# Column-normalised attention with a soft mixture of experts: the last half tile of each batch filled up to 128 partitions

## The chip, the cores and the metric

The kernel runs on one core of one Trainium2 chip. The metric is the device time of one execution in microseconds (us). Of three runs of the kernel before, the median is 304.97 us, the lowest 303.45, the highest 307.35. The time of a kernel is compared with that of the kernel before on the same chip.

## The reference

There are four batches (B) of q, k and v, each with N = 5056 rows and C = 256 columns. In each batch q and k are normalised by column, their product over the rows gives a 256 x 256 matrix, and v times its softmax is the attention's output. That goes through a soft mixture of 8 experts with 4 slots each, whose softmax over rows runs over all batches.

```python
def _attn_ref(q, k, v, tau):
    qn = q / (np.linalg.norm(q, axis=1, keepdims=True) + 1e-06)
    kn = k / (np.linalg.norm(k, axis=1, keepdims=True) + 1e-06)
    s = kn.transpose(0, 2, 1) @ qn / tau
    s = s - s.max(-1, keepdims=True)
    a = np.exp(s)
    a /= a.sum(-1, keepdims=True) + 1e-09
    return (v @ a).astype(np.float32)

def _moe_ref(x, phi, w1, w2):
    logits = x @ phi
    d = softmax of logits over all rows
    slot_input = (d.T @ x).reshape(E, S_per_e, D)
    for e in range(E):
        h = np.maximum(slot_input[e] @ w1[e], 0.0)
        slot_out[e] = h @ w2[e]
    c = softmax of logits over the 32 slots
    return (c @ slot_out).astype(np.float32)
```

Here x is the attention's output of all batches, 20224 rows. 5056 is 39 x 128 + 64: the last tile of 128 rows in a batch is half full.

## The kernel before

**Tiles.** A batch is cut into UB = 10 units of 512 rows for q and k, and into PB = 5 pieces of 1024 rows for v and the output. A unit lies in SBUF as a tile raw of [128 partitions, 4 row tiles, q and k, 256 columns], 1 MB, of which there are five buffers. A piece of v is [128, 8 row tiles, 256], also 1 MB, loaded in two halves of 512 KB. Rows fill the tiles in order, so in the last unit of a batch the fourth row tile has 64 rows instead of 128, and in the last piece of v the eighth.

**Stages.** First, unit by unit: load_qk loads raw; cast (ACT) and low (DVE) split two of its four row tiles into a high and a low part (tile hl); score (PE) adds the products of k and q to two PSUM banks S, with L252 for row tiles read straight from raw and L258 and L259 for split ones; square (ACT) writes the squares to a tile sq, and add (DVE) adds them to the batch's first sq. After a batch's last unit, att_sums and what follows turn the sums into norms, and the softmax a and a small matrix M are made. Meanwhile, piece by piece of the batch before: load_v and load_vt load v and, for some pieces, its transpose; turn (PE) transposes the others; logits, exps, weights and gather run the softmax over rows and gather the slot inputs. Then the experts' weights w1 and w2 are loaded, and up, relu, flip_h, back_h and down run the experts. At the end, piece by piece, out_mul (PE) makes the output in PSUM, out_evict copies it to a tile o of 1 MB (even banks ACT at L791, odd banks DVE at L793), and store writes it to HBM.

**Order.** Every step is entered in a plan, and a list of numbers written out by hand, ORDER, says in what order the steps are given out. Each engine runs its own instructions in that order. All loads and stores are issued on one queue, SP's.

**The half tiles.** The last unit of q and k comes from arrays of its own: L128 loads three row tiles of 128 rows (768 KB, from qk3), L129 the 64 rows (128 KB, from qkh, into partitions 0 to 63 of the fourth). The last half piece of v is loaded by L143 (three row tiles, 384 KB) and L145 (64 rows, 64 KB). The square of such a unit is two instructions (L226 for three row tiles, L227 for the 64 rows), and so is its last sum (L234 and L235). The matmuls of score, gather and turn take `pc = HD` rows there, with HD = 64. In the output the rows of a piece are permuted, so that the half tile of the last piece stands in the first 96 partitions of two of the eight row tiles; out_evict puts these two in the last places of o, and store writes six row tiles of 128 partitions (L804, 768 KB) and two of 96 (L805, 192 KB). The output in HBM is one flat array with a part for full pieces, one for the six and one for the two row tiles; the host puts the rows in order.

Of the kernel before, what the change touches and what calls it, by code (L numbers as in the profile page):

```python
# [8 lines left out]
F32 = mybir.dt.float32  # L9
F32R = mybir.dt.float32r  # L10
AF = mybir.ActivationFunctionType
ALU = mybir.AluOpType
# [3 lines left out]
B, N, C = 4, 5056, 256  # L16
P, S, G = 128, 32, 4
UB = 10
PB = 5
UT = 512  # L20
# [61 lines left out]
def colnorm_attention_soft_moe(  # L82
    ctx: ExitStack,
    tc: tile.TileContext,
    qk: bass.AP,
    qk3: bass.AP,
    qkh: bass.AP,
    v8: bass.AP,
    v7: bass.AP,
    vh: bass.AP,  # L90
    vt8: bass.AP,
    vt7: bass.AP,
    few: bass.AP,
    w1: bass.AP,
    w2: bass.AP,
    oa: bass.AP,
    ob6: bass.AP,
    oh: bass.AP,
):
# [19 lines left out]
    raws, sqs = {}, {}  # L119

    def load_qk(u, parts=((0, 4),)):
        b, i = divmod(u, UB)
        raw = apool.tile([P, 4, 2, C], F32, tag="raw", name=f"raw{u}", bufs=NRAW)
        if i < UB - 1:
            for lo, hi in parts:
                sp.dma_start(raw[:, lo:hi], qk[b, i][:, lo:hi])
        else:
            sp.dma_start(raw[:, 0:3], qk3[b])  # L128
            sp.dma_start(raw[:HD, 3], qkh[b])  # L129
        raws[u] = raw  # L130

    vs, vts = {}, {}
# [1 line left out]
    def load_v(p, h):  # L134
        b, i = divmod(p, PB)
        if p not in vs:
            vs[p] = slot("v" if p < 17 else "raw", f"v{p}")
        vt = vs[p]
        lo, hi = 4 * h, 4 * h + 4
        if i < PB - 1:  # L140
            sp.dma_start(vt[:, lo:hi], v8[b, i][:, lo:hi])
        else:
            sp.dma_start(vt[:, lo : min(hi, 7)], v7[b][:, lo : min(hi, 7)])  # L143
            if h:
                sp.dma_start(vt[:HD, 7], vh[b])  # L145

    def load_vt(p, m):
        b, i = divmod(p, PB)
# [65 lines left out]
    for b in range(B):  # L214
        sqtag[b * UB] = free[0]
        o = free[1:]
# [3 lines left out]

    def square(u):
        sq = apool.tile([P, 4, 2, C], F32, tag=f"sq{sqtag[u]}", name=f"sq{u}")
        if u % UB < UB - 1:
            act.activation(sq, raws[u], AF.Square)  # L224
        else:
            act.activation(sq[:, 0:3], raws[u][:, 0:3], AF.Square)  # L226
            act.activation(sq[:HD, 3], raws[u][:HD, 3], AF.Square)  # L227
        sqs[u] = sq

    def add(u, lo, hi):  # L230
        b, i = divmod(u, UB)
        a, s = sqs[b * UB], sqs[u]
        if i == UB - 1 and hi == 4:
            dve.tensor_tensor(a[:, lo:3], a[:, lo:3], s[:, lo:3], op=ALU.add)  # L234
            dve.tensor_tensor(a[:HD, 3], a[:HD, 3], s[:HD, 3], op=ALU.add)  # L235
        else:
            dve.tensor_tensor(a[:, lo:hi], a[:, lo:hi], s[:, lo:hi], op=ALU.add)  # L237

    def score(u, j):
        b, i = divmod(u, UB)  # L240
# [511 lines left out]
    ots, ops = {}, {}  # L752
# [21 lines left out]
    def out_evict(b, p, hf, g):  # L774
        if (b, p) not in ots:
            ots[b, p] = slot(OT[b * PB + p], f"o{b}_{p}")
        ot = ots[b, p]
        if p < PB - 1:
            dst = ot.rearrange("p q (w c) -> p (q w) c", w=2).rearrange("p (x gh) c -> p gh x c", x=2)
            dst = dst[:, 2 * g : 2 * g + 2]  # L780
            src = ops[b, p, hf, g]
            if hf is None:
                src = src.rearrange("p h (x c) -> p h x c", x=2)
            else:
                dst = dst[:, :, hf]
        else:
            lo, step = (2 * g, 1) if g < 2 else (g + 2, 2)
            dst = ot[:, lo : lo + step + 1 : step, :]
            src = ops[b, p, hf, g]
        if g % 2 == 0:  # L790
            act.copy(dst, src)  # L791
        else:
            dve.tensor_copy(dst, src)  # L793

    def store(b, p, hf):
        ot = ots[b, p]
        if p < PB - 1:
            o2 = ot.rearrange("p (x q) c -> p x (q c)", x=2)
            if hf is None:
                sp.dma_start(oa[b, p], o2)  # L800
            else:
                sp.dma_start(oa[b, p][:, hf], o2[:, hf])
        else:
            sp.dma_start(ob6[b], ot[:, 0:6])  # L804
            sp.dma_start(oh[b], ot[:96, 6:8])  # L805

    def fill(b, k):
        gp = st[b]["gp"]
# [46 lines left out]
    for p in range(14):  # L855
        k = FV + 2 * p
# [5 lines left out]
        b, gi, x, n = group(p)  # L862
# [11 lines left out]
        if p >= 3:  # L874
            at(k + 0.2, gather, p - 3)
            b, gi, x, n = group(p - 3)
# [8 lines left out]
    for b in range(3):  # L885
        k = UB * (b + 1)
# [47 lines left out]
    for p in (17, 18, 19):  # L934
        at(NU + 0.99, load_v, p, 0)
        at(NU + 0.99, load_v, p, 1)
# [193 lines left out]
```

## Time and profile before

| What | us |
|---|---|
| median of three runs | 304.97 |
| the profiled execution | 304.32 |
| its span, first to last instruction | 302.5 |
| PE busy | 260.6 |
| DVE busy | 233.2 |
| ACT busy | 196.1 |

In the span 110.38 MB were moved by DMA, 365 GB/s in the mean. From HBM 89.29 MB were read, and 20.71 MB were written to it. Q and k are loaded from 0.7 to some 180 us, and the stores run from 247.29 us to the end.

How to read the rows: PE is TensorE (PEld its weight loads), DVE VectorE, ACT ScalarE, POOL GpSimd, SP the engine that issues the DMAs (SPq its queue). "S<-raw" is what an instruction writes and reads, by the program's names; "x4" is a count; "L252" a line of the kernel. What stands in brackets at the end of a row is the time for which the engine was idle just before it, and what ended that idle time. PEclk is the clock granted to TensorE as a share of full speed. The DMA share is the mean busy share of 16 DMA engines, and can read a little over 1 where two transfers overlap on an engine.

### The profile page before, as it was taken

The numbers are of one execution on the slowest core, as the hardware profiler recorded it, in microseconds if no ns is written. First come the engines' busy times: TensorE is split into PE (matmuls) and PEld (weight loads), VectorE is DVE, ScalarE is ACT, GpSimd is POOL, SyncE is SP. The second block draws the span as 40 slices with busy tenths as digits, with TensorE's granted clock in tenths as the row PEclk, the third lists the DMA queues.
The fourth block names the chain that finished last, engine by engine and source line by source line (L and its number), as shares of the span: only waits on it lengthen the run. The fifth ranks groups of instructions, "written<-read, shape, count | busy, mean of one in ns | idle before, by whom it ended". The sixth has DMA issues, their size and how long they took to land. (4 is left out here: it accounts for less than half of the span.)

```text
span 302.5 us, 5958 instructions
## 1 busy us (share of the span) xinstructions
PE 260.6 (86%) x2358; PEld 199.4 (66%) x2358; DVE 233.2 (77%) x387; ACT 196.1 (65%) x290; POOL 28.1 (9%) x18
## 2 busy tenths in 40 slices
PE   4999899999999988998999999999989999984000
PEld 3788687877768874875887687777655588763000
DVE  1599959999989979986999999567887547997000
ACT  2996969798879694675886976366840526865000
POOL 0000002000002403000222000133202030000000
PEclk9999799999999999999999999999999999999555
DMA  6999999999999998799899989699999718999996
GB/s 237 427 430 415 374 405 420 371 389 366 423 398 360 417 390 319 280 356 422 281 407 405 385 310 378 248 351 422 406 347 400 305 71 341 404 422 399 420 430 261
DMA packets 21707, 110.38 MB, mean 365 GB/s; under 512 B 2608, under 2 KB 2864, under 8 KB 13616
## 3 DMA queue, kind: packets, MB, share of 16 engines
q1 hardware_dynamic: 21680, 110.01, 92.4%
q8 instruction: 18, 0.29, 0.4%
q14 instruction: 9, 0.07, 0.1%
HBM read 89.29 MB, written 20.71 MB: 364 GB/s over the span
## 5 line engine op out<-in xcount | busy, mean ns | idle before, releaser
L252 PE MATMUL S<-raw 128*128 128x256 f32 (+1 forms) x328 | 82.4, 391 | 6.4 <-DMA raw<-in_qk_dram 4.8
L237 DVE TENSOR_TENSOR sq<-sq,sq 128x1024 f32<-128x1024 f32 (+1 forms) x59 | 81.2, 1393 | 3.2 <-ACT sq L224 2.3
L224 ACT ACTIVATE sq<-raw 128x2048 f32<-128x2048 f32 x36 | 68.7, 1914 | 14.9 <-DMA raw<-in_qk_dram 9.4
L252 PEld LDWEIGHTS S<-raw 128*128 128x128 f32 (+1 forms) x328 | 60.4, 195 | 17.1 <-DMA raw<-in_qk_dram 5.9
L258 PE MATMUL S<-hl 128*128 128x512 f32 x156 | 64.7, 444 | 1.8 <-DVE hl L208 1.8
L208 DVE TENSOR_TENSOR hl<-raw,hl 128x1024 fp32r<-128x1024 f32 x39 | 49.0, 1271 | 8.4 <-ACT hl L202 8.3
L202 ACT CAST hl<-raw 128x1024 fp32r<-128x1024 f32 x39 | 40.4, 1044 | 7.1 <-DMA raw<-in_qk_dram 4.8
L259 PE MATMUL S<-hl 128*128 128x256 f32 x156 | 44.0, 282 | 0.0
L258 PEld LDWEIGHTS S<-hl 128*128 128x128 f32 x156 | 29.6, 190 | 10.5 <-DVE hl L208 2.6
L259 PEld LDWEIGHTS S<-hl 128*128 128x128 f32 x156 | 29.8, 191 | 0.6
L406 PE MATMUL vTp<-ident,v 128*128 128x128 f32 (+1 forms) x160 | 23.4, 277 | 1.7 <-DMA v<-in_v_dram 1.7
L537 PE MATMUL G<-v,dn 128*32 128x256 f32 (+1 forms) x320 | 23.3, 382 | 0.0
L406 PEld LDWEIGHTS vTp<-ident,v 128*128 128x128 f32 (+1 forms) x160 | 18.2, 141 | 6.7 <-issue 3.0
L764 PE MATMUL op_None<-so,cT 32*128 32x256 f32 x256 | 19.6, 397 | 2.3 <-ACT o L791 1.2
L305 POOL TENSOR_TENSOR rn<-rn,half 128x4 f32<-128x4 f32 x4 | 6.8, 1701 | 154.5 <-DVE rn L300 119.8
L793 DVE COPY o<-op_None 128x512 f32<-128x512 f32 x32 | 20.0, 679 | 1.3 <-issue 1.0
L791 ACT COPY o<-op_None 128x512 f32<-128x512 f32 x32 | 17.1, 591 | 5.1 <-PE op_None L764 1.9
L764 PEld LDWEIGHTS op_None<-so,cT 32*128 32x128 f32 x256 | 15.1, 184 | 6.4 <-PE op_None L764 3.2
L428 PE MATMUL L<-vt,M 128*32 128x256 f32 (+1 forms) x272 | 18.2, 381 | 1.1 <-issue 1.1
L413 ACT COPY vt<-vTp 128x512 f32<-128x512 f32 (+1 forms) x28 | 15.8, 576 | 4.0 <-PE vTp L406 2.8
L537 PEld LDWEIGHTS G<-v,dn 128*32 128x32 f32 (+1 forms) x320 | 12.4, 109 | 6.4 <-issue 1.2
L635 POOL TENSOR_TENSOR nat<-nat,cm 128x1280 f32<-128x1280 f32 x4 | 11.2, 2803 | 30.8 <-DVE cm L632 17.5
(119 smaller groups left out, 284.2 us busy)
## 6 DMA issues: line engine op xcount, KB each, us to landing
raw<-in_qk_dram SPq DMA_DIRECT2D x35, 1024.0 KB, 9.1
v<-in_v_dram SPq DMA_DIRECT2D x36, 512.0 KB, 8.3
w<-in_moe_w_dram SPq DMA_DIRECT2D x16, 1024.0 KB, 9.0
out_dram<-o SPq DMA_DIRECT2D x12, 1024.0 KB, 9.5
vt<-in_vt_dram SPq DMA_DIRECT2D x16, 512.0 KB, 9.5
out_dram<-o SPq DMA_DIRECT2D x8, 512.0 KB, 4.1
raw<-in_qk_dram SPq DMA_DIRECT2D x4, 768.0 KB, 8.0
out_dram<-o SPq DMA_DIRECT2D x4, 768.0 KB, 8.0
```

The costliest lines, as they stand in the source:

```text
L202: act.copy(hl[:, :ns, 0::2, :], raws[u][:, :ns])
L208: dve.tensor_tensor(hl[:, :ns, 1::2, :], raws[u][:, :ns], hl[:, :ns, 0::2, :].bitcast(F32), op=ALU.subtract)
L224: act.activation(sq, raws[u], AF.Square)
L237: dve.tensor_tensor(a[:, lo:hi], a[:, lo:hi], s[:, lo:hi], op=ALU.add)
L252: pe.matmul(sm[:, :C], raw[:pc, j, 1, cols], raw[:pc, j, 0, :], start=first, stop=False, skip_group_check=True)
L258: pe.matmul(sm, hl[:, j, 2, cols], rhs, start=first, stop=False, skip_group_check=True)
L259: pe.matmul(sm[:, :C], hl[:, j, 3, cols], hl[:, j, 0, :], start=False, stop=False, skip_group_check=True)
L406: pe.transpose(tp[:, n : n + pc], vs[p][:pc, 4 * h + jj, P * m : P * m + P], ident[:pc, :pc])
L428: pe.matmul(L[S * g : S * g + S, :n, :], M[:, m, :], x[:, :n, S * g : S * g + S], start=m == 0, stop=m == 1,)
L537: pe.matmul(gp[S * g : S * g + S, :C], dn[:pc, x, j, :], vt[:pc, j, :], start=x == 0 and j < G, stop=x == n - 1 and j >= G,)
L764: pe.matmul(ops[b, p, hf, g][:, h, :], cT[b][S * g : S * g + S, 4 * i : 4 * i + 4, :].rearrange("s j t -> s (j t)"), so[S * g : S * g + S] ...
L793: dve.tensor_copy(dst, src)
```

## The change

The host now puts q and k of all ten units in one array that is filled up with zero rows, 5120 rows a batch, and v likewise. Load_qk loads the last unit as any other, in one DMA of 1024 KB; load_v loads the last half piece in one DMA of 512 KB. Square and add treat the last unit as any other; zero rows add nothing to the sums. The matmuls keep their `pc = HD`, and the transposes of v, loaded or made on PE, keep their length. Out_evict copies the last piece in the arrangement of the others, and store writes it in one DMA of 1024 KB, with rows that belong to nothing and that the host cuts off. The output array is [4, 5, 128, 2, 1024].

```diff
     def load_qk(u, parts=((0, 4),)):
...
-        if i < UB - 1:
-            for lo, hi in parts:
-                sp.dma_start(raw[:, lo:hi], qk[b, i][:, lo:hi])
-        else:
-            sp.dma_start(raw[:, 0:3], qk3[b])
-            sp.dma_start(raw[:HD, 3], qkh[b])
+        for lo, hi in parts:
+            sp.dma_start(raw[:, lo:hi], qk[b, i][:, lo:hi])
...
-        if i < PB - 1:
-            sp.dma_start(vt[:, lo:hi], v8[b, i][:, lo:hi])
-        else:
-            sp.dma_start(vt[:, lo : min(hi, 7)], v7[b][:, lo : min(hi, 7)])
-            if h:
-                sp.dma_start(vt[:HD, 7], vh[b])
+        sp.dma_start(vt[:, lo:hi], v8[b, i][:, lo:hi])
...
-        if u % UB < UB - 1:
-            act.activation(sq, raws[u], AF.Square)
-        else:
-            act.activation(sq[:, 0:3], raws[u][:, 0:3], AF.Square)
-            act.activation(sq[:HD, 3], raws[u][:HD, 3], AF.Square)
+        act.activation(sq, raws[u], AF.Square)
...
-        if i == UB - 1 and hi == 4:
-            dve.tensor_tensor(a[:, lo:3], a[:, lo:3], s[:, lo:3], op=ALU.add)
-            dve.tensor_tensor(a[:HD, 3], a[:HD, 3], s[:HD, 3], op=ALU.add)
-        else:
-            dve.tensor_tensor(a[:, lo:hi], a[:, lo:hi], s[:, lo:hi], op=ALU.add)
+        dve.tensor_tensor(a[:, lo:hi], a[:, lo:hi], s[:, lo:hi], op=ALU.add)
...
-        else:
-            lo, step = (2 * g, 1) if g < 2 else (g + 2, 2)
-            dst = ot[:, lo : lo + step + 1 : step, :]
-            src = ops[b, p, hf, g]
...
-        else:
-            sp.dma_start(ob6[b], ot[:, 0:6])
-            sp.dma_start(oh[b], ot[:96, 6:8])
...
+    x = np.zeros((B, UB * UT, 2, C), np.float32)
+    x[:, :N, 0], x[:, :N, 1] = q, k
+    add("qk", x.reshape(B, UB, 4, P, 2, C).transpose(0, 1, 3, 2, 4, 5))
+    n4 = 4 * 2 * UT
+    x = np.zeros((B, UB * UT, C), np.float32)
+    x[:, :N] = v
+    add("v8", x.reshape(B, PB, 8, P, C).transpose(0, 1, 3, 2, 4))
...
+    out_ap = nc.dram_tensor("out_0_dram", (B, PB, P, 2, 4 * C), F32, kind="ExternalOutput").ap()
```

In the built program PE's and POOL's instructions stand as before; SP has twelve DMAs less, ACT four squares less, DVE four sums less. SP's queue at the end of batch 1, before (raw_553 is the batch's last unit, v_503 the last piece of batch 0's v):

```order
L126 DMA raw_547<-in_qk_dram 128x2048
L126 DMA raw_551<-in_qk_dram 128x2048
L128 DMA raw_553<-in_qk_dram 128x1536
L129 DMA raw_553<-in_qkh_dram 64x512
L143 DMA v_503<-in_v_dram 128x768
L145 DMA v_503<-in_vh_dram 64x256
L141 DMA v_595<-in_v_dram 128x1024 x2
L151 DMA vt_0_631<-in_vt_dram 128x1024
```

And the same place after (raw_550 and v_500 are the same tiles; the lines' numbers are those of the changed kernel):

```order
L119 DMA raw_544<-in_qk_dram 128x2048
L119 DMA raw_548<-in_qk_dram 128x2048
L119 DMA raw_550<-in_qk_dram 128x2048
L130 DMA v_500<-in_v_dram 128x1024
L130 DMA v_590<-in_v_dram 128x1024 x2
L136 DMA vt_0_626<-in_vt_dram 128x1024
```

Four DMAs have become two, in the same place among the others.

SP's queue at the end of the program, before (o_4_2925 is the last piece of the last batch):

```order
L800 DMA out_dram<-o_2_2888 128x2048
L800 DMA out_dram<-o_0_2754 128x2048
L800 DMA out_dram<-o_3_2910 128x2048
L804 DMA out_dram<-o_4_2925 128x1536
L805 DMA out_dram<-o_4_2925 96x512
L1116 UNCONDITIONAL_BRANCH
```

And after:

```order
L771 DMA out_dram<-o_2_2869 128x2048
L771 DMA out_dram<-o_0_2737 128x2048
L771 DMA out_dram<-o_3_2891 128x2048
L771 DMA out_dram<-o_4_2906 128x2048
L1072 UNCONDITIONAL_BRANCH
```

The last two stores have become one.

More of the change, by code (lines that the diff above doesn't have):

```diff
@@ L96, in colnorm_attention_soft_moe @@
     oa: bass.AP,
-    ob6: bass.AP,
-    oh: bass.AP,
 ):
@@ L777, in out_evict @@
         ot = ots[b, p]
-        if p < PB - 1:
-            dst = ot.rearrange("p q (w c) -> p (q w) c", w=2).rearrange("p (x gh) c -> p gh x c", x=2)
-            dst = dst[:, 2 * g : 2 * g + 2]
-            src = ops[b, p, hf, g]
-            if hf is None:
-                src = src.rearrange("p h (x c) -> p h x c", x=2)
-            else:
-                dst = dst[:, :, hf]
-        else:
-            lo, step = (2 * g, 1) if g < 2 else (g + 2, 2)
-            dst = ot[:, lo : lo + step + 1 : step, :]
-            src = ops[b, p, hf, g]
+        dst = ot.rearrange("p q (w c) -> p (q w) c", w=2).rearrange("p (x gh) c -> p gh x c", x=2)
+        dst = dst[:, 2 * g : 2 * g + 2]
+        src = ops[b, p, hf, g]
+        if hf is None:
+            src = src.rearrange("p h (x c) -> p h x c", x=2)
+        else:
+            dst = dst[:, :, hf]
         if g % 2 == 0:
@@ L796, in store @@
         ot = ots[b, p]
[L797 to L800, printed above, removed]
-            else:
-                sp.dma_start(oa[b, p][:, hf], o2[:, hf])
-        else:
-            sp.dma_start(ob6[b], ot[:, 0:6])
-            sp.dma_start(oh[b], ot[:96, 6:8])
+        o2 = ot.rearrange("p (x q) c -> p x (q c)", x=2)
+        if hf is None:
+            sp.dma_start(oa[b, p], o2)
+        else:
+            sp.dma_start(oa[b, p][:, hf], o2[:, hf])
     def fill(b, k):
@@ L1103 @@
         add(name, inputs[name])
-    flat = nc.dram_tensor("out_0_dram", (B * N * C,), F32, kind="ExternalOutput").ap()
-    cuts = np.cumsum([0, B * 4 * P * 8 * C, B * P * 6 * C, B * 96 * 2 * C])
-    shapes = [(B, 4, P, 2, 4 * C), (B, P, 6, C), (B, 96, 2, C)]
-    pats = [
[3 rows of a table removed]
-    ]
-    for x_, (lo, hi) in enumerate(zip(cuts[:-1], cuts[1:])):
-        sh = shapes[x_]
-        names = pats[x_].split("->")[1].split()
-        args.append(flat[int(lo) : int(hi)].rearrange(pats[x_], **dict(zip(names[1:], sh[1:]))))
+    out_ap = nc.dram_tensor("out_0_dram", (B, PB, P, 2, 4 * C), F32, kind="ExternalOutput").ap()
+    args.append(out_ap)
     with tile.TileContext(nc, schedule_with_timeline_sim=True) as tc:
@@ L1118 @@
     r = run_bass_kernel_spmd(nc, [arrays], core_ids=[0])
-    o = np.asarray(r.results[0]["out_0_dram"]).reshape(-1)
-    oa, ob, oh = (o[int(lo) : int(hi)].reshape(sh) for lo, hi, sh in zip(cuts[:-1], cuts[1:], shapes))
-    out = np.empty((B, N, C), np.float32)
-    out[:, :n4] = oa.reshape(B, 4, 4, S, 2, G, 2, P).transpose(0, 1, 6, 2, 5, 3, 4, 7).reshape(B, n4, C)
-    last = np.zeros((B, P, 8, C), np.float32)
-    last[:, :, [0, 1, 2, 3, 4, 6]] = ob
-    last[:, :96, [5, 7]] = oh
-    last = last.reshape(B, 4, S, G, 2, C).transpose(0, 4, 1, 3, 2, 5)
-    out[:, n4:] = last.reshape(B, 2 * UT, C)[:, : N - n4]
+    o = np.asarray(r.results[0]["out_0_dram"]).reshape(B, PB, 4, S, 2, G, 2, P)
+    out = o.transpose(0, 1, 6, 2, 5, 3, 4, 7).reshape(B, UB * UT, C)[:, :N]
     return out.reshape(B * N, C)
```

13 lines of the change are left out of this document (removed), and 3 rows, old and new, of the table pats.

## The prediction

> **What bounds the kernel now.** I read the page first, then the busy times by stage, then the end of the program in order of time, then the waits around the half tiles.
>
> ```profile
> span 302.5 us, 5958 instructions
> PE 260.6 (86%) x2358; PEld 199.4 (66%) x2358; DVE 233.2 (77%) x387; ACT 196.1 (65%) x290; POOL 28.1 (9%) x18
> ...
> DMA  6999999999999998799899989699999718999996
> ```
>
> Two resources are nearly full: TensorE and the DMA engines. An average can't say which of them sets the time, so the stages stand apart here (each row: the stretch, its length, busy time of PE, weight loads, DVE, ACT, POOL, granted clock, DMA share, GB/s):
>
> ```profile
> core 0: us, PE busy (x) PEld busy (x) DVE busy (x) ACT busy (x) POOL busy (x), PEclk, DMA share, GB/s
> 10.00:110.00 100.00, 97.69 (x607) 79.01 (x606) 91.29 (x110) 84.44 (x93) 7.13 (x3) 0.98 1.01 399
> 110.00:200.00 90.00, 84.87 (x673) 64.30 (x671) 80.02 (x130) 61.98 (x88) 10.53 (x5) 1.00 0.91 343
> 200.00:240.00 40.00, 38.27 (x436) 24.20 (x440) 30.98 (x77) 22.10 (x56) 7.39 (x4) 1.00 0.98 398
> 240.00:249.00 9.00, 9.00 (x250) 7.46 (x242) 3.64 (x10) 2.46 (x7) 2.35 (x1) 1.00 0.13 52
> 249.00:255.00 6.00, 5.65 (x135) 4.99 (x133) 3.69 (x11) 3.38 (x11) 0.00 (x0) 1.00 0.76 305
> 255.00:301.00 46.00, 19.51 (x264) 14.99 (x257) 22.36 (x40) 17.80 (x35) 0.00 (x0) 0.77 0.99 404
> ```
>
> Up to 240 us PE works 94 to 98 of 100 us, and the DMA engines fill nearly all of the same time: the loads run ahead of a PE that hardly stops. From 240 to 249 us only the expert layers run. From 255 us on it is the other way round: PE works 19.5 of 46 us and the DMA engines 99%. There the stores are the bound, to the last of them:
>
> ```profile
> 285.56 1.19 SPq L804 DMA_DIRECT2D out_dram<-o  x1
> 286.80 1.23 SPq L805 DMA_DIRECT2D out_dram<-o  x1
> ```
>
> The last store was issued at 286.80 us and the span ends at 302.5: some 14 us of stores are queued when SP has nothing left to issue. So bytes and transfer rate count in full after 255 us, and before 240 us only where PE really waits for a load.
>
> **The change, part by part: the stores.** Issues of whole and of partial tiles (bytes of one, median us from issue to landing):
>
> ```profile
> out_dram<-o SPq DMA_DIRECT2D x12, 1024.0 KB, 9.5
> ...
> raw<-in_qk_dram SPq DMA_DIRECT2D x4, 768.0 KB, 8.0
> out_dram<-o SPq DMA_DIRECT2D x4, 768.0 KB, 8.0
> ...
> out_dram<-o SPq DMA_DIRECT2D x4, 192.0 KB, 7.6
> ...
> raw<-in_qkh_dram SPq DMA_DIRECT2D x4, 128.0 KB, 8.1
> v<-in_vh_dram SPq DMA_DIRECT2D x4, 64.0 KB, 6.9
> ```
>
> Four pairs of 768 + 192 KB become four stores of 1024 KB: 64 KB more each, 4 x 65.5 kB = 262 kB. Against it stands the rate at which the pairs go. The trace by stretches, clean ones beside those that hold partial tiles (33 to 39 us is for later):
>
> ```profile
> 20.00:27.00 7.00, 7.00 (x37) 5.98 (x36) 6.95 (x5) 5.44 (x5) 0.00 (x0) 1.00 1.02 426
> 29.00:33.00 4.00, 3.02 (x16) 2.39 (x14) 4.00 (x4) 2.86 (x3) 0.00 (x0) 1.00 1.03 344
> 33.00:39.00 6.00, 5.52 (x18) 4.37 (x19) 6.00 (x4) 5.46 (x5) 0.00 (x0) 0.72 1.02 418
> 69.00:74.00 5.00, 5.00 (x37) 3.73 (x36) 4.78 (x5) 3.73 (x6) 0.00 (x0) 1.00 1.03 345
> 274.00:278.00 4.00, 2.21 (x33) 1.44 (x25) 3.07 (x5) 2.86 (x6) 0.00 (x0) 1.00 1.01 399
> 278.00:282.00 4.00, 0.00 (x0) 0.00 (x0) 0.70 (x2) 0.01 (x1) 0.00 (x0) 0.77 1.03 404
> 286.00:290.00 4.00, 0.00 (x0) 0.00 (x0) 0.00 (x0) 0.00 (x0) 0.00 (x0) 0.50 1.02 430
> ```
>
> A full queue moves about 426 GB/s. The two pairs issued between 271 and 275 us pass through the queue from 274 to 282 us, at 399 and 404 GB/s: (27 + 22) x 4 us = 196 kB less than a clean queue moves, or 0.46 us, 0.23 us a pair. If the filled stores go at the clean rate, the four dips go (-0.92 us) and the extra bytes come (262 kB / 426 = +0.62 us): -0.30 us. If the dips have another cause, it is +0.62 us. I take -0.30, because the full tiles behind these pairs go at 430. The four stores less on SP cost nothing either way: 14 us are queued behind it.
>
> **The loads.** The q and k pair of a batch grows by 131 kB, the v pair by 65.5 kB: 4 x 196.6 = 786 kB, or 1.85 us at 426 GB/s. The rate dips here as well: 29 to 33 us, with batch 0's q and k pair, ran at 344 GB/s, (82 x 4) / 426 = 0.77 us; 69 to 74 us, with batch 1's pair and the first v pair, at 345, (81 x 5) / 426 = 0.95 us. Less the extra bytes (0.31 and 0.46 us) that is -0.46 and -0.49 us, if the dips go with the partial tiles. PE, though, is what most of this would have to reach, and it waited for a half tile just once:
>
> ```profile
> 33.48 0.70 PE L252 MATMUL S<-raw 64*128 64x256 f32 x2 [1.46 <-DMA raw<-in_qkh_dram]
> ...
> 76.96 1.08 PE L252 MATMUL S<-raw 64*128 64x256 f32 x4
> ...
> 130.07 1.13 PE L252 MATMUL S<-raw 64*128 64x256 f32 x4
> ...
> 182.47 0.62 ACT L227 ACTIVATE sq<-raw 64x512 f32<-64x512 f32 x1
> ...
> 185.62 1.08 PE L252 MATMUL S<-raw 64*128 64x256 f32 x4
> ```
>
> At 33.48 us batch 0's half tile came 1.46 us late. This is the one place where an earlier landing moves PE, by at most 0.46 us. I take -0.2, about half, since the 8 KB rows of other loads were in the same queue and may be the slow part. In the other batches PE comes to the half tile without a DMA wait, so their bytes are hidden by loads that run ahead; that cover is gone if a landing moves by more than some 3 us (batch 3: ACT reads the half tile at 182.47, PE at 185.62). Together the loads lie between -1.1 (all dips gone, all of it on the path) and +1.85 us (no dip goes, every byte on the path).
>
> **ScalarE, VectorE and SP.** Split instructions become one. Min, median and max ns where there are three numbers, else the mean:
>
> ```profile
> L224 ACT ACTIVATE sq<-raw 128x2048 f32<-128x2048 f32 x36 | 68.7, 1914 | 14.9 <-DMA raw<-in_qk_dram 9.4 <-DVE sq L237 5.5
> ...
> L226 ACT ACTIVATE sq<-raw x4: 1479/1484/1489, 37.2 to 181.1; 128x1536 f32<-128x1536 f32 x4
> L227 ACT ACTIVATE sq<-raw x4: 617/618/619, 38.6 to 182.5; 64x512 f32<-64x512 f32 x4
> ...
> L234 DVE TENSOR_TENSOR sq<-sq,sq x4: 649/680/1753, 43.2 to 183.5; 128x512 f32<-128x512 f32 x3, 128x1536 f32<-128x1536 f32 x1
> L235 DVE TENSOR_TENSOR sq<-sq,sq x4: 673/674/683, 44.9 to 184.1; 64x512 f32<-64x512 f32 x4
> L237 DVE TENSOR_TENSOR sq<-sq,sq 128x1024 f32<-128x1024 f32 x51 | 62.9, 1252 | 2.5 <-ACT sq L224 1.7 <-ACT sq L226 0.5
> ...
> L791 ACT COPY o<-op_None x32: 585/592/606, 256.1 to 277.4; 128x512 f32<-128x512 f32 x32
> ```
>
> ACT saves 1.484 + 0.618 - 1.914 = 0.19 us a batch, DVE 0.680 + 0.674 - 1.252 = 0.10 us: 0.75 and 0.4 us in all, on engines that PE's work covers (ACT is busy 62 of 90 us from 110 to 200 us). I count nothing, and -0.4 as the bound. One square now waits for the whole tile instead of its first three quarters; the 131 kB that this adds are 0.31 us, inside the 3 us. Output copies change the shape they write, yet both shapes are among the 32 copies of 585 to 606 ns: nothing. PE's own instructions stay: the matmuls still read 64 rows.
>
> On SP the eight small loads and four small stores go:
>
> ```profile
> L129 SPq DMA_DIRECT2D raw<-in_qkh_dram x4: 471/506/762, 23.1 to 176.7; - x4
> ...
> L145 SPq DMA_DIRECT2D v<-in_vh_dram x4: 471/472/472, 67.3 to 183.7; - x4
> ...
> L805 SPq DMA_DIRECT2D out_dram<-o x4: 1229/1285/1882, 257.9 to 286.8; - x4
> ```
>
> That is 4 x (0.506 + 0.472 + 1.285) = 9.1 us of SP. What is queued behind them are later loads with a landing time of 8 to 9 us, most of it queue, and stores behind a full queue; no engine waits for SP's issue as such. I count 0.
>
> How much of a DMA's fixed time shows, the trace answers: 192 KB land in 7.6 us and 1024 KB in 9.5, but while they do, the engines are 99% busy with their neighbours. The Trainium skill (DMA: Bandwidth & Descriptors, section Anatomy of one DMA) gives some 2.0 us fixed for each DMA beside its bytes, fitted for DMAs that GpSimd issues; twelve DMAs less would by that be worth 24 us, an estimate from that page, and a time near 281 us. The row from 255 to 301 us speaks against adding these up, since nothing in it is idle for 2 us between DMAs.
>
> **The sum.** -0.30 (stores) - 0.2 (loads) + 0 = -0.5 us. The profiled execution took 304.32 us, 1.8 more than its span, so it would take 303.8. It stands 0.65 us under the median of the runs, 304.97; on that median the forecast is 304.5 us, and the cases below are on the median too.
>
> **The rivals.**
>
> (B) Bytes in full. The dips are not the partial tiles' doing, and the DMA engines bound the kernel before 240 us too: +0.62 + 1.85 = +2.5 us, 307.4. For it speaks the DMA share of 1.01 from 10 to 110 us; against it, PE's 97.69 of 100 us there.
>
> (C) A PE stall less. Batch 0's tile lands 0.46 us earlier, and with a shorter stall the low clock after it does not come: from 33 to 39 us the granted clock averaged 0.72, so (1 - 0.72) x 6 = 1.7 us of PE work were lost. With the stores: -0.30 - 0.46 - 1.7 = -2.5 us, 302.5. Against it: a wait of 1 us is left. The Trainium skill (TensorE: Matmul & The Clock Gate, Part 1) says that the clock is set by free-running windows of about 3.4 us; 0.72 over 6 us is one such window at half speed, so the trace agrees, and it leaves open whether 1 us is short enough.
>
> (D) Slower: a stall in every batch. The single load holds back the three quarters that came first, and PE stands in batches 1 to 3 as it stood in batch 0: 1.46 us and 1.7 us of low clock each, 3 x 3.16 = +9.5 us, 314.5. It decides from a landing that comes over 3.1 us later (185.62 less 182.47); the extra bytes make 0.31.
>
> (E) SP's queue sets the pace, or each DMA's own time counts: the 9.1 us of issues come off, 295.9. Against it are the full DMA engines.
>
> That the change misses its aim is no case: the built program has twelve DMAs less, all with 128 partitions.
>
> **How the numbers follow.** The forecast, between 303 and 306.5, gets 0.72, B 0.12, C 0.10, D 0.03, E 0.03. The time is the forecast's, 304.5. The range runs from C's 302.5, widened to 302.3 for the spread of the runs, to B's 307.4; D and E lie outside it. Two per cent, about what a measurement of this kernel can tell from no change, is 6.1 us: E alone is faster by more (0.03), D alone slower (0.03), and the rest, 0.94, is within.
>
> **What would show it.** The clean rate of some 425 GB/s without a dip where a batch's last store passes would prove the store term; dips that stay prove B's half of it. The first wait of PE on batch 0's last tile, now on one load, shows the load term: shorter than 1.46 us for mine, gone with a full clock for C. New waits of PE on q and k loads near 77, 130 or 185 us would mean D. A start of the stores earlier than 247 us by more than 1 us would say that something before 240 us was worth more than I gave it. A span whose stores end more than 1 us earlier at the same start would make the store term wrong.

## The result, and the profile after

| | median, us | lowest to highest | runs |
|---|---|---|---|
| before | 304.85 | 301.88 to 307.35 | 20 |
| the change | 307.50 | 304.71 to 309.29 | 20 |

The ratio is 1.0113, with a 95% interval of 1.0086 to 1.0140: about 1% slower, less than the two per cent that would count as a change, and 0.1 us beyond the upper end of the range. The profiled execution of the change took 308.21 us. (The ratios in this document leave out executions more than 1.5% above the fastest of their kernel, which takes more from a kernel whose executions spread more, so the median of all stands beside each ratio.)

From the page of the change (span; busy time of each engine, its share and its instructions):

```profile
span 306.4 us, 5935 instructions
...
PE 263.1 (86%) x2358; PEld 199.8 (65%) x2358; DVE 233.2 (76%) x383; ACT 195.8 (64%) x286; POOL 28.1 (9%) x18
```

The span is 3.9 us longer, and PE's busy time 2.5 us; DVE and ACT are where they were. So PE's work takes longer, and PE stands longer. The next view tells where: SP's first store, and the issue of the last q and k load, in order of time (start, length, instruction), first of the change:

```profile
174.74 0.33 SPq L119 DMA_DIRECT2D raw<-in_qk_dram  x1
...
251.36 0.35 SPq L773 DMA_DIRECT2D out_dram<-o  x1
```

and of the kernel before:

```profile
176.29 0.33 SPq L128 DMA_DIRECT2D raw<-in_qk_dram  x1
...
247.29 2.01 SPq L802 DMA_DIRECT2D out_dram<-o  x2
```

At 175 us the changed kernel is 1.55 us ahead. At its first store it is 4.07 us behind. From there to the end both need the same but for 0.2 us (306.4 - 251.36 = 55.0, and 302.5 - 247.29 = 55.2). So the stages on either side of 175 us gained, and some 5.6 us were lost in between. The busy times by stage of the change (stretch, its length, PE, weight loads, DVE, ACT, POOL, granted clock, DMA share, GB/s) show what was gained and where the loss lies:

```profile
29.00:33.00 4.00, 2.99 (x15) 2.07 (x13) 4.00 (x3) 2.56 (x2) 0.00 (x0) 1.00 1.00 421
33.00:39.00 6.00, 6.00 (x29) 5.02 (x30) 6.00 (x4) 5.81 (x5) 0.00 (x0) 1.00 1.02 422
69.00:74.00 5.00, 5.00 (x39) 3.75 (x38) 4.79 (x7) 4.13 (x5) 0.00 (x0) 1.00 1.01 376
180.00:185.00 5.00, 2.81 (x16) 2.23 (x15) 2.57 (x3) 2.70 (x3) 0.00 (x0) 1.00 0.99 334
185.00:190.00 5.00, 5.00 (x19) 3.10 (x18) 2.74 (x3) 2.23 (x4) 0.00 (x0) 0.59 1.03 420
190.00:195.00 5.00, 5.00 (x39) 2.77 (x38) 3.16 (x9) 1.20 (x2) 0.00 (x0) 0.73 0.10 37
276.00:280.00 4.00, 3.03 (x41) 2.22 (x41) 3.72 (x7) 2.98 (x6) 0.00 (x0) 1.00 1.01 418
280.00:284.00 4.00, 0.82 (x14) 0.41 (x6) 2.02 (x4) 1.56 (x3) 0.00 (x0) 1.00 1.01 424
290.00:294.00 4.00, 0.00 (x0) 0.00 (x0) 0.00 (x0) 0.00 (x0) 0.00 (x0) 0.50 1.01 426
```

The dips in the rate are gone where partial tiles used to pass: 421 instead of 344 GB/s at 29 us, 418 and 424 instead of 399 and 404 in the stores, a clean queue at 290 us has 426, and at 69 us, with 376 instead of 345, the dip is less than half gone. The low clock from 33 to 39 us (0.72 before) is gone too. The loss is two rows: from 180 to 185 us PE works 2.81 of 5 us, and from 185 to 195 us it runs at a clock of 0.59 and 0.73, which costs (0.41 + 0.27) x 5 = 3.4 us. The wait itself, in order of time, after:

```profile
182.30 1.91 ACT L208 ACTIVATE sq<-raw 128x2048 f32<-128x2048 f32 x1 [2.90 <-DMA raw<-in_qk_dram]
184.11 1.06 ACT L390 COPY vt<-vTp 128x512 f32<-128x512 f32 x2
...
184.73 0.65 PE L383 MATMUL vTp<-ident,v 128*128 128x128 f32 x4 [2.19 <-ACT vt L390]
```

and before:

```profile
181.08 1.48 ACT L226 ACTIVATE sq<-raw 128x1536 f32<-128x1536 f32 x1 [1.18 <-DMA raw<-in_qk_dram]
...
182.99 1.04 ACT L413 COPY vt<-vTp 128x512 f32<-128x512 f32 x2
...
183.95 0.60 PE L406 MATMUL vTp<-ident,v 128*128 128x128 f32 x4
```

ACT waits for batch 3's last q and k load, to square it. Behind the square in ACT's queue stand the copies that empty PE's banks of transposed v (vTp). PE's next transposes need a bank, and wait 2.19 us for a copy whose own input had long been there (the transposes before these were made at 177.09). 2.19 + 3.4 = 5.6 us: that is the whole loss of this execution.

It is not the loss of the median. The mean granted clock of each execution is on record: it averages 0.955 over the twenty of the change, and 0.955 to 0.957 over the kernel before in the four later series of runs (134 executions). So the change does not run at a lower clock on the average. Span times clock, an estimate of the time at full clock (it also takes out the low clock of the last 20 us or so, where PE has little to do), averages 292.0 us for the change and 289.7 to 290.1 for the kernel before: some 2 us more, about the size of PE's wait.

The load itself, from issue to landing, is what moved, after and before:

```profile
  ACT sq L208: 2.9, 1
...
DMA to landing us min/median/max: 7.5/7.5/7.5
```

```profile
  ACT sq L226: 1.2, 1
...
DMA to landing us min/median/max: 4.7/4.7/4.7
```

2.8 us later, for 33% more bytes.

### The profile page after: what moved, and what is told of

Read it like the earlier page. It is cut to its first block, busy times and chain, and to the rows that moved or that the text cites. A ratio compares the mean times of both kernels' runs of the same rounds, so it can differ in the third digit from the quotient of the medians.

```text
span 306.4 us, 5935 instructions
## 1 busy us (share of the span) xinstructions
PE 263.1 (86%) x2358; PEld 199.8 (65%) x2358; DVE 233.2 (76%) x383; ACT 195.8 (64%) x286; POOL 28.1 (9%) x18
## 5 line engine op out<-in xcount | busy, mean ns | idle before, releaser
L214 DVE TENSOR_TENSOR sq<-sq,sq 128x1024 f32<-128x1024 f32 (+1 forms) x63 | 87.0, 1398 | 5.6 <-ACT sq L208 5.2
L208 ACT ACTIVATE sq<-raw 128x2048 f32<-128x2048 f32 x40 | 76.3, 1914 | 17.2 <-DMA raw<-in_qk_dram 12.5
L235 PE MATMUL S<-hl 128*128 128x512 f32 x156 | 64.0, 440 | 1.1 <-DVE hl L193 1.1
L405 PE MATMUL L<-vt,M 128*32 128x256 f32 (+1 forms) x272 | 19.2, 396 | 1.8 <-PE n L255 0.9
L405 PEld LDWEIGHTS L<-vt,M 128*32 128x32 f32 x272 | 8.1, 112 | 9.3 <-issue 1.9
```

Source lines behind the costliest of these rows:

```text
L235: pe.matmul(sm, hl[:, j, 2, cols], rhs, start=first, stop=False, skip_group_check=True)
L405: pe.matmul(L[S * g : S * g + S, :n, :], M[:, m, :], x[:, :n, S * g : S * g + S], start=m == 0, stop=m == 1,)
```

## The experiments

All times are medians of all executions, in us; "before" is the kernel before on the same chip in the same series of runs.

| kernel | median (range, n) | before | ratio (95%) |
|---|---|---|---|
| qk_only | 303.51 (301.33 to 305.02, 12) | 304.98 | 0.9943 (0.9909 to 0.9977) |
| v_out | 304.75 (303.78 to 306.11, 12) | 304.98 | 0.9995 (0.9967 to 1.0024) |
| split39 | 305.15 (303.36 to 307.00, 12) | 304.98 | 1.0013 (0.9981 to 1.0046) |
| late_sq | 308.09 (303.98 to 310.17, 12) | 304.98 | 1.0085 (1.0039 to 1.0130) |
| after_again | 306.17 (303.97 to 309.25, 10) | 304.35 | 1.0022 (0.9979 to 1.0065) |
| mid_sq | 304.03 (301.45 to 305.43, 12) | 304.35 | 1.0007 (0.9968 to 1.0046) |
| v14_before | 303.70 (301.81 to 307.33, 12) | 304.35 | 0.9962 (0.9923 to 1.0001) |
| qk_out | 303.71 (301.58 to 307.05, 12) | 304.35 | 0.9937 (0.9898 to 0.9976) |
| plus1 | 307.45 (301.92 to 310.20, 6) | 304.87 | - |
| plus3 | 306.67 (303.18 to 310.00, 12) | 304.87 | 1.0057 (1.0015 to 1.0098) |
| mid_before | 304.18 (302.26 to 308.64, 12) | 304.87 | 0.9991 (0.9958 to 1.0025) |
| qk_out_mid | 303.45 (301.57 to 306.88, 12) | 304.87 | 0.9980 (0.9942 to 1.0019) |
| v14_back | 304.53 (301.95 to 308.05, 12) | 305.29 | 0.9971 (0.9930 to 1.0011) |
| v9_before | 306.12 (303.82 to 309.14, 12) | 305.29 | 1.0014 (0.9972 to 1.0056) |
| v14_only | 305.71 (303.39 to 309.46, 12) | 305.29 | 1.0017 (0.9976 to 1.0058) |
| v14_split | 306.86 (302.29 to 309.97, 12) | 305.29 | 0.9982 (0.9935 to 1.0029) |

### One part of the change at a time: qk_only and v_out

qk_only is the kernel before with q and k alone filled up (load, square and sums as in the change); v_out is the kernel before with v and the output alone filled up.

```diff
 # qk_only: in load_qk
...
-            sp.dma_start(raw[:, 0:3], qk3[b])
-            sp.dma_start(raw[:HD, 3], qkh[b])
...
+            sp.dma_start(raw[:, lo:hi], qk[b, i][:, lo:hi])
...
 # v_out: in load_v (out_evict and store are those of the change)
...
-            sp.dma_start(vt[:, lo : min(hi, 7)], v7[b][:, lo : min(hi, 7)])
...
-                sp.dma_start(vt[:HD, 7], vh[b])
+        sp.dma_start(vt[:, lo:hi], v8[b, i][:, lo:hi])
...
```

> Before with q and k alone filled up: one load of 1024 KB for a batch's last unit, one square, whole sums; v and the output as before. Theory one (in batch 3 the square on ACT waits for the whole load of the last unit, the copies of transposed v queue behind it, PE stalls about 2 us and its clock falls): nearly all of the loss is here, ratio to before 1.008 to 1.013. Theory two (the added bytes count in full): 0.52 of 1.05 MB, ratio about 1.004, half of the change's loss or less.

> Before with v and the output alone filled up; q and k in their two loads, two squares, two sums. Theory one: no loss, the ratio to before is 0.997 to 1.002, with the stores 0 to 0.3 us shorter. Theory two: 0.52 MB more, ratio about 1.004 to 1.006.

qk_only is faster, by 1.5 us, where both theories had it slower; v_out is the same, as theory one had it. Neither part is the loss by itself; it takes both. In qk_only, in order of time, PE's wait of batch 0 is the shorter one, and no wait stands ahead of the transposes of v:

```profile
32.98 1.13 PE L238 MATMUL S<-raw 64*128 64x256 f32 x4 [0.73 <-DMA raw<-in_qk_dram]
...
182.80 0.65 PE L392 MATMUL vTp<-ident,v 128*128 128x128 f32 x4
```

The load's line:

```profile
DMA to landing us min/median/max: 5.1/5.1/5.1
```

Against 4.7 us before, that is what the bytes alone add (131 kB at 426 GB/s would be 0.31 us).

### The load or the queue behind it: split39, late_sq and mid_sq

split39 is the change with the last q and k load in two DMAs of 768 and 256 KB, and two squares:

```diff
+        if u == NU - 1:
+            parts = ((0, 3), (3, 4))
...
+            act.activation(sq[:, 0:3], raws[u][:, 0:3], AF.Square)
+            act.activation(sq[:, 3], raws[u][:, 3], AF.Square)
```

> The changed kernel, with only batch 3's last unit loaded in two DMAs (three row tiles of 128 partitions, 768 KB, then one, 256 KB) and squared in two instructions; the bytes are those of the change. Theory one: the first square starts before 181.5 us, PE has no stall of over 1 us near 183 us, and the time falls by 2 to 5 us against the change: ratio to before 0.990 to 1.002. Theory two: same bytes, so as slow as the change, ratio 1.008 to 1.013.

305.15, by its ratio as fast as the kernel before, which is what theory one gave; the two signs that it gave for the profile did not come. PE's wait halves but doesn't go, since the first of the two DMAs is late as well (its square starts 6.4 us after the issue at 175.46, against 181.08 - 176.29 = 4.8 us before):

```profile
181.83 1.49 ACT L211 ACTIVATE sq<-raw 128x1536 f32<-128x1536 f32 x1 [2.01 <-DMA raw<-in_qk_dram]
...
184.36 0.66 PE L389 MATMUL vTp<-ident,v 128*128 128x128 f32 x4 [1.09 <-ACT vt L396]
```

So it isn't the joining of the two loads into one that makes the load late; whatever is late is late for both parts. The joining has a share in what the lateness costs: with the load in two parts, and the square with it, the time is that of the kernel before again.

late_sq and mid_sq are the change with another order: the square of that unit (step 369) and its sums (371 and 370) go behind all four copies of transposed v (late_sq; the expectation counts three, the profile shows four), or between the first two and the last two (mid_sq). Nothing is removed or added. (The numbers of ORDER from 359 to 415, without the line breaks of the kernel.)

```diff
 # mid_sq, in ORDER; late_sq has the three behind 415
-    359, 369, 361, 371, 355, 345, 676, 677, 370, 413, 362, 682, 411, 683, 346, 414, 415,
+    359, 361, 355, 345, 676, 677, 413, 362, 682, 411, 369, 371, 370, 683, 346, 414, 415,
```

> The changed kernel, with the square and the sums of batch 3's last unit given out after three copies of transposed v (turned 13, 14 and 15) instead of ahead of them; loads and bytes as in the change. Theory one: the copies no longer wait for the load, PE's stall near 183 us goes, ratio to before 0.990 to 1.003. Theory two: ratio 1.008 to 1.013. If the late landing itself held PE (its matmuls on the half tile), it would stay as slow as well.

> The changed kernel with the square of batch 3's last unit between the first two and the last two of the four copies of transposed v on ACT (the run with the square behind all four moved the stall to the sums). Theory one: the stall goes and none takes its place, ratio 0.990 to 1.000. Theory three: as slow as the change, 1.007 to 1.014.

late_sq missed: 308.09, as slow as the change. The wait had only moved. Where the copies no longer stand behind the square, the norms do: PE's sums of the squares, some 3 us on, now wait for it, through DVE (the instruction that ends PE's wait, L566, stands right behind the sums in DVE's queue).

```profile
184.20 2.36 DVE L212 TENSOR_TENSOR sq<-sq,sq 128x1024 f32<-128x1024 f32 x2 [3.61 <-ACT sq L206]
...
186.99 1.41 PE L253 MATMUL n<-sq,ones 128*32 128x512 f32 x8 [2.23 <-DVE acc L566]
```

Its profiled execution, of 304.09 us, is the second shortest of twelve (ten took 307.36 to 310.17), so its profile shows the mechanism but not the price. mid_sq strikes between the two consumers, and there the loss is gone: 304.03, with every byte of the change and a load that is as late as ever.

```profile
178.63 1.06 ACT L388 COPY vt<-vTp 128x512 f32<-128x512 f32 x2
181.57 1.92 ACT L206 ACTIVATE sq<-raw 128x2048 f32<-128x2048 f32 x1 [1.87 <-DMA raw<-in_qk_dram]
...
181.92 0.60 PE L381 MATMUL vTp<-ident,v 128*128 128x128 f32 x4
...
188.79 1.06 PE L381 MATMUL vTp<-ident,v 128*128 128x128 f32 x8 [0.89 <-DMA v<-in_v_dram]
```

and the load's line:

```profile
DMA to landing us min/median/max: 7.2/7.2/7.2
```

ACT still waits for a load that takes 7.2 us, but the copies are done, and the transposes at 181.92 wait for nothing. Later, at 188.79, 0.89 us are lost on a load of v. The slowest of mid_sq's twelve executions, 305.43, is below six of the ten of after_again on the same chip, and below 18 of the 20 of the first comparison. (The ratios of mid_sq and after_again, 1.0007 and 1.0022, can't be told apart; the means of all their executions, 303.97 and 306.29 us, are 2.3 us apart.)

after_again is the change once more, beside these.

> The changed kernel once more, for a second profile beside those below. Theory one, as the first four runs left it: the loss is a PE stall at batch 3's end, because the last unit's load lands late there and the copies of transposed v wait behind its square on ACT; the stall of about 2 us near 183 us shows again, time ratio 1.007 to 1.014. Theory three (the profile's stall was chance, the loss is spread over many waits or lies in the low clock): no PE stall over 1 us between 180 and 190 us, ratio still 1.007 to 1.014.

306.17, 1.8 us above the kernel before where the first comparison had 2.65; its ratio, 1.0022, lies below what either theory gave, and by it alone the difference would not be established on this chip. Its profiled execution (309.25, its slowest) has the same wait, 2.38 us, as theory one had it, and another of 2.84 us at 143 us that ends with nothing the profile names.

The same move in the kernel before (mid_before) and in the fastest version (qk_out_mid, below) is the control: if the order were better as such, they would gain as mid_sq does.

> The kernel before with the last unit's squares moved between the copies of transposed v, as in the run that took the stall out of the changed kernel. Theory one: before has no stall there, so the move brings nothing, ratio 0.996 to 1.004. If the move is simply a better order and has nothing to do with the change: ratio 0.989 to 0.995.

> Q, k and the output filled, v as before, with the square moved between the copies: the version that should be the fastest. Theory one: the 0.6 us stall of the run without the move goes, ratio 0.988 to 0.996. If nothing is left to gain there: 0.993 to 0.998.

Neither gains anything that the measurement can tell (0.9991 and 0.9980, against qk_out's 0.9937 in another series); qk_out_mid missed what theory one gave it. In mid_before's profile the load landed after 4.8 us, so there was no wait to remove. In qk_out_mid's it landed late, after 6.9 us, and PE's transposes, at 181.24 us, had no wait. The move is worth something only where the load is late often enough to show in the median.

### Which load ahead makes it late: qk_out, v14_before, plus1, plus3

qk_out is the change with v as before. v14_before has all filled up but one load: the last half piece of batch 2's v (piece 14), which is issued some 9 us ahead of the late load (at 165.42 us in the change, the late load at 174.74). plus1 and plus3 are the change with one or three other loads of q and k (units 22, or 15, 22 and 26) split in two, so that the number of DMAs ahead changes and nothing else.

```diff
 # v14_before: in load_v
+        if p != 14 or h == 0:
             sp.dma_start(vt[:, lo:hi], v8[b, i][:, lo:hi])
+        else:
+            sp.dma_start(vt[:, lo:7], v7[b][:, lo:7])
+            sp.dma_start(vt[:HD, 7], vh[b])
 # plus1: in load_qk; plus3 has (15, 22, 26)
+        if u in (22,):
+            parts = ((0, 2), (2, 4))
```

> The changed kernel with all of v in its loads of before; q, k and the output filled. If it is the filled v beside the filled q and k that costs (theory one with a late landing): about as the kernel with q and k alone filled, less 0.3 us of stores, ratio 0.990 to 0.997. If the stores or the output cost: 1.005 or more.

> The changed kernel with the last half piece of batch 2's v alone in its two loads of before (64 KB less, one DMA more, issued some 10 us ahead of batch 3's last q and k load). If the bytes just ahead make that load late: the stall shrinks, ratio 0.995 to 1.004. If they do not: 1.007 to 1.014.

> The changed kernel with unit 22's load (batch 2, some 75 us before the stall) in two DMAs of two row tiles each: the same bytes, one DMA more ahead of batch 3's last q and k load. In five profiles of kernels with q, k and all of v filled that load landed 6.3 to 7.7 us after its issue; in four with q and k or v in small loads, 4.7 to 5.9. Theory place (the landing depends on where in the queue's count of DMAs it stands, not on bytes): it lands in under 6.3 us, PE's stall near 185 us is under 1 us, ratio 0.990 to 1.002. Theory bytes: lands in 6.3 us or more, stall 1.5 us or more, ratio 1.002 to 1.014.

> The same with three units' loads in two DMAs each (15, 22 and 26): the same bytes, three DMAs more ahead of the load, about the count that the kernel with q, k and the output filled has there. Theory place: landing under 6.3 us, stall under 1 us, ratio 0.990 to 1.002. Theory bytes: as the change, 1.002 to 1.014.

qk_out, at 303.71 and 0.9937, is as fast as qk_only: v is what must not be filled up beside q and k. v14_before, with one small load put back, was as fast in the median, 303.70, but its profile, of its slowest execution (307.33), had the late landing of 7.0 us all the same. Splitting other loads did not help: plus1 is inconclusive (six executions, 301.92 to 310.20, and in its profile the landing of 6.0 us and the wait of 0.73 that theory place gave), plus3 is slow at 306.67 with a landing of 7.1 us. So more DMAs ahead do not bring the time back.

Four more kernels asked whether this one load is the cause: v14_back is v14_before again, v9_before puts back batch 1's instead, v14_only fills up only this one of the four (with q, k and output), and v14_split loads it filled up, in two DMAs of 384 and 128 KB.

```diff
 # v9_before / v14_only, in place of p != 14
+        if p != 9 or h == 0:
+        if p not in (4, 9, 19) or h == 0:
 # v14_split: in the change's load_v
+        if p == 14 and h == 1:
+            sp.dma_start(vt[:, lo:7], v8[b, i][:, lo:7])
+            sp.dma_start(vt[:, 7], v8[b, i][:, 7])
```

> The change with one load alone put back: the last half piece of v of batch 2 (piece 14, issued some 8 us ahead of the last q and k load) goes as 384 KB and 64 KB of 64 partitions; all else is filled up. It was 303.70 in the median before, but its one profile, of an execution of 307.3, had the late landing of 7.0 us. Theory one (this load, just ahead in the queue, decides the landing): again 303.2 to 304.3, and in a profile of an execution near the median the last q and k load lands within 6.0 us and PE's wait for the copies is under 0.8 us. Theory two (no single place decides; the landing is late in some executions of every kernel with v filled up): 305 to 307, landing over 6.5 us.

> The same with another load put back: the last half piece of v of batch 1 (piece 9), some 50 us earlier; piece 14 stays filled up. Theory one: as slow as the change, 305.8 to 307.5, landing over 6.5 us, PE's wait over 1.2 us. Theory two: as the kernel with piece 14 put back, within 0.7 us of it.

> The turn of it: q, k and output filled up, of v the last half piece of batch 2 alone; those of batches 0, 1 and 3 as before. Theory one: this one filled load brings the loss back, 305.8 to 307.5 against 303.7 with v wholly as before, landing over 6.5 us, PE's wait over 1.2 us. Theory two: between, nearer 303.7 than 306.2, with a landing under 6.5 us.

> The change, all filled up, with the last half piece of v of batch 2 loaded by two DMAs of 128 partitions, 384 KB and 128 KB. The bytes are those of the change, the number of DMAs is that of the kernel with this load put back. If the number of DMAs ahead in the queue decides: 303.2 to 304.3 and a landing within 6.0 us. If the bytes or the 64 partitions decide: 305.8 to 307.5 and a landing over 6.5 us.

The times lean to this one load, nearly as theory one had them: medians of 304.53 with it put back, and 306.12, 305.71 and 306.86 with it filled up; means of all executions of 304.70, and 306.17, 306.09 and 306.61. V14_before and after_again had stood the same way round (means of 303.98 and 306.29). The intervals of the ratios overlap, though, and the profiles don't fall in line with what theory one gave. v14_only's has the late landing (in order of time, then the load's line):

```profile
181.68 1.91 ACT L214 ACTIVATE sq<-raw 128x2048 f32<-128x2048 f32 x1 [2.13 <-DMA raw<-in_qk_dram]
...
184.12 0.66 PE L389 MATMUL vTp<-ident,v 128*128 128x128 f32 x4 [2.46 <-ACT vt L396]
```

```profile
DMA to landing us min/median/max: 7.7/7.7/7.7
```

v14_split's, with the same bytes in the queue, hasn't:

```profile
183.56 0.66 PE L387 MATMUL vTp<-ident,v 128*128 128x128 f32 x4
```

```profile
DMA to landing us min/median/max: 5.2/5.2/5.2
```

and v9_before's (an execution of 303.82, its fastest) lands after 5.5 us. v14_before and v14_back are one program, with 7.0 us in an execution of 307.33 and 5.7 in one of 302.50. So the landing is no fixed property of a kernel: it differs from execution to execution. With one profile a kernel, the eighteen landings stand like this: with q and k as before, 4.7, 4.8 and 5.0 us; with q and k filled up and v as before, 5.1, 5.9 and 6.9; with some of v filled up as well, 5.5, 5.7, 7.0 and 7.7; with all of it, 5.2 to 7.7, six of the eight at 6.3 or more. The late ones seem to grow more frequent with what is filled up, and qk_out_mid's 6.9 shows that they don't need a filled v. Why is not settled. The neighbour in the queue is a candidate that the times favour and the intervals don't prove.

### What all the profiles agree on

The landing of that load and PE's wait at the transposes behind the copies, in the thirteen profiles in which the order is the change's own and the load goes in one DMA, or in before's two (there, the first):

| kernel | landing, us | PE's wait, us | landing less wait |
|---|---|---|---|
| before | 4.7 | 0 | |
| v_out | 5.0 | 0 | |
| qk_only | 5.1 | 0 | |
| v14_split | 5.2 | 0 | |
| v9_before | 5.5 | 0.24 | 5.3 |
| v14_back | 5.7 | 0.44 | 5.3 |
| qk_out | 5.9 | 0.61 | 5.3 |
| plus1 | 6.0 | 0.73 | 5.3 |
| v14_before | 7.0 | 1.70 | 5.3 |
| plus3 | 7.1 | 1.80 | 5.3 |
| the change | 7.5 | 2.19 | 5.3 |
| after_again | 7.7 | 2.38 | 5.3 |
| v14_only | 7.7 | 2.46 | 5.2 |

Up to 5.3 us the landing costs PE nothing; beyond, all of it. The kernel before stood at 4.7: at most 0.6 us from the edge.

## Why the prediction was wrong, by its steps

**The stores: right.** -0.30 was forecast. From first store to the end of the span, the three profiles with pairs of stores (before, qk_only and mid_before) need 55.25, 55.24 and 55.70 us, in the mean 55.40; the fifteen with whole ones need 54.81 to 55.56, in the mean 55.04: -0.36 us (-0.19 from before to the change). The dips were the partial tiles', as assumed. Rival E had no part in it: the first store came later, and four stores less were worth some 0.3 us.

**Batch 0's load: right in kind, too small.** At most 0.46 us off the wait was forecast; 0.73 came off:

```profile
32.94 1.13 PE L229 MATMUL S<-raw 64*128 64x256 f32 x4 [0.73 <-DMA raw<-in_qk_dram]
```

It is 0.71 to 0.73 in thirteen of the fifteen profiles with q and k filled up (0.27 in split39, none in late_sq). The low clock behind it, 0.28 x 6 = 1.7 us of the profile before, is gone as well, as rival C had it. That is no gain to count on, though: v_out, whose wait stayed at 1.45 us, has no low clock there either (its rows are at the end). Of the 2.4 us, 1.55 were left at 175 us. qk_only, without the loss later on, was 1.5 us faster in the median: more than the 0.73. Its executions ran at a mean clock of 0.960, the kernel before's at 0.955, which on some 302 us is 1.6 us; but qk_out, with the same loads of q and k, ran at 0.957, so this is nothing to count on either. (The -1.1 us that the prediction names as the lower end for the loads does not come out of its two rows, -0.46 - 0.49 = -0.95; neither its sum nor its range uses it.)

**ScalarE, VectorE and SP: right, as far as work goes.** ACT's and DVE's busy times moved by 0.3 us or less, and no wait of PE is put down to SP. What ACT waits for is another matter, and the next point.

**The step that failed is the cover of the other batches' loads, in both of its terms.** The first term is the landing. The prediction let it move by the bytes alone ("the 131 kB that this adds are 0.31 us"). It moved by 2.8 us, from 4.7 to 7.5; in qk_only, where this load has the same bytes, by 0.4.

The second term is the slack. The prediction gave it "some 3 us (batch 3: ACT reads the half tile at 182.47, PE at 185.62)" and put the single square "inside the 3 us". That is the slack of the matmul that reads the load. But ACT reads it first, in order, and what stands behind the square in ACT's queue are the copies that PE needs. The slack on that way was 0.3 to 0.6 us, and it could have been read off before. The copies followed the square at once (182.47 + 0.62, then 182.99), and the transposes began at 183.95, 0.96 us behind the start of the copies; in the change, where they waited for them, they began 0.62 behind it (184.73 after 184.11). That makes 0.3 us; the table's edge makes 0.6. The Trainium skill (TensorE: Matmul & The Clock Gate, section on the array's architecture) says that the queues of ScalarE and VectorE are strictly first in, first out; the copies at 184.11, behind a square that had waited 2.90 us, agree.

Either term alone would have cost nothing: 0.4 us of delay hardly touched the true slack (qk_only has no wait there), and 2.8 us would have stayed within a slack of 3.

**Rival D was right in mechanism and wrong in place, point of decision and count.** The one load does hold back PE, with a low clock behind it. It does so through ACT's copies, not by PE's own read; from a delay of 0.3 to 0.6 us on, not 3.1; and in batch 3 alone, not in batches 1 to 3. The price was 2.19 us of wait, and 3.4 of low clock that belong to the profiled execution and not to the average one. The chance of 0.03 rested on the point of 3.1 us, and was far too small.

**Rival B gave nearly the right time, 307.4, by luck, for a wrong reason.** Bytes in full would make qk_only slower (it is 1.5 us faster), v_out slower, and mid_sq, with all the bytes, 2.5 us slower (it is 304.03, where the kernel before has 304.35). The bytes cost next to nothing.

**What stays open** is why the last load comes so late with both filled up. The bytes explain 0.4 us of the 2.8 (qk_only). The trace keeps the moment at which each of the 16 DMA engines reports its share of this load as done, and that shows where the rest lies. In eight profiles (before, the change, after_again, qk_only, v14_only, v14_split, v14_back, v9_before) the first engine is done 3.6 to 4.4 us after the issue, late landing or not. The last is done 0.9 to 1.6 us after the first in the five early landings, and 3.0 to 3.6 us after it in the three late ones (the change, after_again, v14_only). In the change fourteen engines are done by 5.8 us, and the last two at 7.3 and 7.5; in qk_out_mid fifteen are done by 4.7, and the last at 6.9; in v14_only five come after 6.7. So a few engines come late, not the load as a whole. Which engines they are the records don't say, and what holds them back was not found.

The fastest version is the change without v: qk_out, with q, k and output filled up, 0.9937 (0.9898 to 0.9976), or qk_only at 0.9943, which can't be told from it.

## What to carry to other kernels

A load's slack is that of its first reader and of everything queued behind that reader on its engine, not that of the matmul which reads it last: here 0.3 to 0.6 us instead of 3. Before two transfers are joined or made longer, follow the reader's queue to the next instruction that another engine waits for; if a late load can't be avoided, let what is ready go first, as mid_sq did, but see who waits for the reader's result, as late_sq did not. And try the parts of a change alone: v, which by itself changed nothing, turned the gain of q and k into a loss.

## What the hardware showed that was not expected

**A wait of PE and the low clock behind it come apart.** A wait of 1.46 us (before) was followed by a clock of 0.72 over 6 us, one of 2.19 us (the change) by 0.59 and 0.73 over 5 us each. A wait of 1.45 us at the same place as the first (v_out) was followed by none, and one of 2.38 us (after_again) by none either. V_out:

```profile
33.87 0.48 PE L243 MATMUL S<-raw 64*128 64x256 f32 x1 [1.45 <-DMA raw<-in_qkh_dram]
...
33.00:39.00 6.00, 5.13 (x25) 4.27 (x25) 6.00 (x4) 6.00 (x6) 0.00 (x0) 1.00 1.01 412
```

After_again, whose wait ended at 186.89 us:

```profile
185.00:190.00 5.00, 3.11 (x18) 2.35 (x19) 3.50 (x3) 4.10 (x6) 0.00 (x0) 1.00 1.02 416
190.00:195.00 5.00, 5.00 (x47) 3.46 (x45) 3.92 (x10) 2.59 (x6) 0.00 (x0) 1.00 0.44 179
```

The Trainium skill (TensorE: Matmul & The Clock Gate, Part 1) has free-running windows of some 3.4 us decide the clock, so that a like wait may or may not fall badly; these runs agree with that, and the clock's own records have half speed for 3.4 us behind the wait in before and for 6.8 in the change. So the 1.7 or 3.4 us of a profile are no price to count on: one execution has them and the next has not, and on the average the change's clock is no lower than before's.

**A load's landing differs by 1.3 us between two executions of one program** (7.0 and 5.7 us, v14_before and v14_back), and it is the slowest of the 16 DMA engines that spreads, not the first. A slack below that can't be counted on.
